# Sliding-window attention and soft MoE: value rows loaded two to a packet, keys ordered odd then even

## The chip, the cores and the metric

The kernel runs on one core of a Trainium2 chip. The metric is device time in microseconds (us) of one execution; lower is better. The engines are called as the profile calls them: PE (TensorE matmul) and PEld (its weight loads), DVE (VectorE), ACT (ScalarE), POOL (GpSimd) and SP (SyncE).

## The reference

Attention over 8 batches of 8 heads, 576 positions and 64 dimensions, in which a query sees itself and the 63 keys before it, then a soft mixture of 8 experts with 4 slots each on the 4608 tokens.

```python
scores = scale * np.matmul(q, k.transpose(0, 1, 3, 2))
mask = (rel >= 0) & (rel < window)            # window = 64
scores = np.where(mask, scores, -1000000000.0)
...
attn = attn / (np.sum(attn, axis=-1, keepdims=True) + 1e-09)
return np.matmul(attn, v).astype(np.float32)
...
logits = x @ phi                              # x: the attention's output, 4608 x 512
d = ...                                       # softmax of logits over tokens
slot_input = d.T @ x
...
h = np.maximum(slot_input[e] @ w1[e], 0.0)    # 512 -> 1024
slot_out[e] = h @ w2[e]                       # 1024 -> 512
c = ...                                       # softmax of logits over slots
return c @ slot_out
```

## The kernel before, in words

**Pairs and blocks.** Two heads of a batch are a pair; there are 32 pairs (`NP`), four to a batch. A head's 576 queries are nine blocks of 64. Block i sees the 128 keys of a window that begins 64 before the block (`kwindow`, L344). The two heads of a pair lie on partitions 0 to 63 and 64 to 127: `qb` holds the queries with zeros for the other head, so that one product with 128 weight columns gives the scores of both.

**A step of the main loop** (L556 to L635) works on several pairs at different stages, all in an order written out by hand (`manual_schedule`); every engine runs its own instructions in that order. For step n: scores of block 8 of pair n-3 (`st_score8`); transposes of the keys of pair n+1 (L319) and their copy into `kT` (`st_copy_k`, on ACT at L330, for every fourth pair on DVE at L327); attention times values of pair n-4 (`st_av`, L408) and its division (L417, L418); transposes and copies of the queries of pair n; the maxima by query (L349, L352 in PE; L356, L366 in DVE), which become an extra row of weights `rt` (L369, L370); transposes of the attention's output (`fr_transpose`, L432); scores of blocks 0 to 7 of pair n-2 by key (`st_score`: first L375, keys as weights and queries streamed, then L378, which adds mask and maximum) and the exponential (L384). Once in four steps come the logits, the softmax over tokens and the slots of a batch (`fr_logits`, `fr_dispatch`, `fr_slots`, `fr_acc`).

**The shape of a product.** A form such as 128*64 128x65 in the profile is: 128 rows and 64 columns of weights, 65 columns streamed. The transposes (96*64) and the value products (128*64) alternate between the lower and the upper 64 output partitions; scores and maxima are 128*128.

**Values.** Two pairs are a group (16 groups). `load_v` puts 18 chunks of 128 key rows of a group into `v1`, one row (64 values, float32 to float16 on the way) to a partition. For every second window the chunk boundaries lie 64 rows off; for these `shift_v` has POOL copy the two halves of each chunk into `v2` (L183, L185). A column of ones behind the values gives the sum of the weights.

**Loads.** K, q, v and most weights are loaded by DMAs that POOL issues, in the order of its instructions. In step n = 2i `loads` first takes a weight load if one is due (`WSLOTS`), then waits for and shifts the values of group i-1, then issues v of group i+1 and q of group i+3; in step 2i+1 it issues k of group i+4. POOL also does a subtraction for the softmax over slots once in four steps (L491). At the end of the loop it issues the last weights: w1 of expert 7 into the buffers of q, then the halves of w2 of experts 6 and 7 (`load_half`, L150 and L155; w2 of 6 has a tile of its own, w2 of 7 lies in the buffers of k).

**The end.** After the last pair come the slots, the first expert products (`first`, L819), the second (`second` L840, `second_last` L849, which uses the halves last loaded), and the output: products with the softmax over slots (L896), a scaling (L901, L903), and 16 stores from SP's queue (L905).

Of the kernel before, what the change touches and what calls it, by code (L numbers as in the profile page):

```python
# [12 lines left out]
ALU = mybir.AluOpType  # L13
# [5 lines left out]
def kernel(  # L19
# [21 lines left out]
    NFC = F // 128  # L41
    NRES = E - 1
    NCH = H * S // 128
    VP = 96

    ctx.enter_context(tc.manual_schedule())

# [42 lines left out]
    w1_t, w2_t = {}, {}  # L90
    for e in range(NRES):
        w1 = pwt.tile([128, NKK, F], FP16, name=f"w1_{e}")
        w2 = pwt.tile([128, NFC, D], FP16, name=f"w2_{e}")
        w1_t[e] = [w1[:, kk, :] for kk in range(NKK)]
        w2_t[e] = [w2[:, fc, :] for fc in range(NFC)]
        w1_t[e, 0], w2_t[e, 0] = w1, w2


    first_rows = {}
# [9 lines left out]
    def round_rows(tag, pr, copy):  # L109
# [1 line left out]

    ident_h = const.tile([128, 128], FP16, name="ident_h")
    nc.vector.memset(ident_h, 0.0)
    wb = const.tile([64, 128], FP16, name="wb")
    nc.vector.memset(wb, 0.0)
    make_identity(nc, ident_h, nomemset=True)
    nc.gpsimd.affine_select(out=wb, in_=wb, compare_op=ALU.is_gt, fill=NEG,
                            base=0, pattern=[[1, 128]], channel_multiplier=-1)
    nc.gpsimd.affine_select(out=wb, in_=wb, compare_op=ALU.is_ge, fill=NEG,
                            base=64, pattern=[[-1, 128]], channel_multiplier=1)  # L120
    load_k(1)


# [43 lines left out]
    v1s = [pvv.tile([128, NCH, VP], FP16, name=f"v1_{i}") for i in range(2)]  # L167
    v2s = [pvv.tile([128, NCH, 66], FP16, name=f"v2_{i}") for i in range(2)]

    def load_v(g):  # L170
        b, gq = divmod(g, 2)
        c = slice(NVC * gq, NVC * gq + NVC)
        nc.gpsimd.dma_start(out=v1s[b % 2][:, c, 0:Dh],  # L173
                            in_=v[b].rearrange("h s d -> (h s) d").rearrange("(c p) d -> p c d", p=128)[:, c, :])

    def shift_v(g):
        b, gq = divmod(g, 2)
        v1, v2 = v1s[b % 2], v2s[b % 2]
        c0, c1 = NVC * gq, NVC * gq + NVC

        w1, w2 = [t[:, :, :].rearrange("p c x -> p (c x)").bitcast(mybir.dt.int32)
                  .rearrange("p (c x) -> p c x", c=NCH)[:, :, 0:Dh // 2] for t in (v1, v2)]
        nc.gpsimd.tensor_copy(out=w2[64:128, c0:c1, :], in_=w1[0:64, c0:c1, :])  # L183
        c0 = max(c0, 1)
        nc.gpsimd.tensor_copy(out=w2[0:64, c0:c1, :], in_=w1[64:128, c0 - 1:c1 - 1, :])  # L185


    warm = v1s[1][:, 0:7, :].rearrange("p c x -> p (c x)")
    nc.vector.memset(warm, 1.0)

    def warm_up(n):
# [22 lines left out]
    nc.scalar.copy(out=lh[64:128], in_=db[64:128, 0:NB].unsqueeze(2).broadcast_to([64, NB, 128]))  # L214

    NK, NQ = 4, 3
    kTs = [pqk.tile([128, 64 + S], FP16, name=f"kT{i}") for i in range(NK)]
    qbs = [pqk.tile([128, NB, 2, 64], FP16, name=f"qb{i}") for i in range(NQ)]
    def zero_q(i):
        nc.vector.memset(qbs[i][64:128, :, 0, :], 0.0)  # L220
        nc.vector.memset(qbs[i][0:64, :, 1, :], 0.0)

    for t_ in kTs:
        nc.vector.memset(t_[:, 0:64], 0.0)
    zero_q(0)

    def no_token():
# [1 line left out]

    no_token()  # L230
    round_rows("ks", 0, nc.scalar.copy)
    nc.vector.tensor_copy(out=lh[0:64], in_=wb[:, :].unsqueeze(1).broadcast_to([64, NB, 128]))
    round_rows("qs", 0, nc.vector.tensor_copy)
    wm = const.tile([128, 5, 128], FP16, name="wm")
    for i in range(2):
        nc.vector.tensor_copy(out=wm[64 * i:64 * i + 64], in_=wb[:, :].unsqueeze(1).broadcast_to([64, 5, 128]))
    nc.vector.memset(wm[:, 0, 0:64], NEG)
    round_rows("ks", 1, nc.vector.tensor_copy)
    NR = 2
    rts = [const.tile([128, 128], FP16, name=f"rt{i}") for i in range(NR)]  # L240
# [7 lines left out]
    ms = [const.tile([128, 128], FP16, name=f"m{i}") for i in range(2)]  # L248

    def ones_v(i):  # L250
        nc.vector.memset(v1s[i][:, :, Dh:Dh + 1], 1.0)
        nc.vector.memset(v2s[i][:, :, Dh:Dh + 1], 1.0)
        nc.vector.memset(v2s[i][0:64, 0, 0:Dh], 0.0)


    phi_f = w1_t[NRES - 1, 0][:, 0, 0:2 * NKK * NSLOT].bitcast(FP32).rearrange("p (c s) -> p c s", s=NSLOT)
# [4 lines left out]
    ssf = const.tile([128, 4, 32], FP32, name="ssf")  # L261
    quarter = const.tile([128, 4], FP32, name="quarter")
    emask = const.tile([128, 2], FP32, name="emask")

    def late_constants(n):
        if n == 0:
            nc.vector.memset(ms[0], 0.0)
            zero_q(1)
        elif n == 1:
            nc.vector.tensor_tensor(out=lh[64:128, 0, 0:64], in0=lh[64:128, 0, 0:64],  # L270
                                    in1=db[64:128, 10:11].broadcast_to([64, 64]), op=ALU.add)
            make_rt(rts[0])
            nc.vector.memset(ms[1], 0.0)
            zero_q(2)
        elif n == 2:
            make_rt(rts[1])
        elif n == 3:
            ones_v(0)
        elif n == 4:
            ones_v(1)  # L280
        elif n == 5:
            nc.vector.tensor_copy(out=phi_sb, in_=phi_f)
            nc.vector.memset(quarter, 0.0)
            for d_ in ds:
                nc.vector.memset(d_[:, 192:256], 0.0)
            nc.vector.memset(nmax[1], 1.0e30)
            nc.vector.memset(stat, 0.0)
        elif n == 7:
            for t in range(4):
                nc.vector.tensor_copy(out=ss[32 * t:32 * t + 32],  # L290
                                      in_=ident_h[32 * t:32 * t + 32, 32 * t:32 * t + 32]
                                      .unsqueeze(1).broadcast_to([32, 4, 32]))
                nc.vector.memset(quarter[32 * t:32 * t + 32, t:t + 1], 1.0)
        elif n == 15:
            nc.vector.tensor_copy(out=ssf, in_=ss)
# [26 lines left out]
    def turned(tq):  # L322
        return tq[:, 0:S].rearrange("p (r g) -> p g r", r=RQ)

    def st_copy_k(p, on_vector=False):
        if on_vector:
            nc.vector.tensor_scalar(out=kTs[p % NK][:, 64:64 + S], in0=turned(a_kh), scalar1=QKS, scalar2=None,  # L327
                                    op0=ALU.mult)
        else:
            nc.scalar.activation(kTs[p % NK][:, 64:64 + S], turned(a_kh), AF.Copy, scale=QKS)  # L330

    def st_copy_q(p, both=False):
        for hf in range(2):
# [38 lines left out]
    def st_scores(p, blocks, at):  # L372
        rt = rts[p % NR]
        for i in blocks:
            nc.tensor.matmul(at(i), kwindow(p, i), qblock(p, i), start=(i % 4 == 0), stop=False,  # L375
                             skip_group_check=True)
        for i in blocks:
            nc.tensor.matmul(at(i), lh[:, i, :], rt[:, :], start=False, stop=True, skip_group_check=True)  # L378

# [19 lines left out]
    def st_av(p, a_v=a_v):  # L399
        b, hp = divmod(p, HP)  # L400
        v1, v2 = v1s[b % 2], v2s[b % 2]
        pt = pts.pop(p)
        for hf in range(2):
            for i in range(NB):
                f = NB * (2 * hp + hf) + i
                rhs = (v1 if f % 2 else v2)[:, f // 2, 0:65]
                r0 = 64 * (i % 2)
                nc.tensor.matmul(a_v[r0:r0 + 64, hf, 65 * (i // 2):65 * (i // 2) + 65],  # L408
                                 pt[:, i, 64 * hf:64 * hf + 64], rhs, start=True, stop=True, skip_group_check=True)
# [132 lines left out]
    def loads(n):  # L542
        if n in WSLOTS:
            load_w(WSLOTS[n])
        i, odd = divmod(n, 2)
        if odd:
            if 0 <= i < NG - 4:
                load_k(i + 4)
        elif i > 0:
            shift_v(i - 1)  # L550
            if i + 1 < NG:
                load_v(i + 1)
            if i + 3 < NG:
                load_q(i + 3)

    for n in range(-1, NP - 1):  # L556
        loads(n)
# [80 lines left out]
    def fill(k, bank):  # L638
        for _ in range(k):
# [2 lines left out]


    NE = 2 * S // 128
    ct4 = [v1s[0][:, 12 * i:12 * i + 12, :].rearrange("p c x -> p (c x)").rearrange("p (e x) -> p e x", e=NE)
           for i in range(3)]
    v2f = v2s[0][:, :, :].rearrange("p c x -> p (c x)")
    ct4.append(v2f[:, 0:2 * S].rearrange("p (e x) -> p e x", e=NE))
# [89 lines left out]
    fr_exp(b - 1)  # L738
    fr_transpose_copy(p - 2, a_qh)
    nc.vector.memset(a_s[:, 0, 128:192], -1.0e30)  # L740
    st_av(p)
    st_norm(p)
    th = a_mh[:, 1, 0:256]
    fr_dispatch(b - 1, th)
# [19 lines left out]
    ssf_ = ssf[:, :, :].rearrange("p t s -> p (t s)")  # L764
# [22 lines left out]
    accs = kTs[0][:, 0:D]  # L787
# [182 lines left out]
```

## Time and profile before

| | |
|---|---|
| three timed runs | median 191.71 us (190.43 to 192.57) |
| the profiled execution | 190.24 us, of which the span from the first to the last instruction is 188.2 us |
| granted TensorE clock, mean | 0.978 |
| DMA packets | 62,302, of which 38,848 under 512 B; 41.47 MB, mean 220 GB/s |
| HBM | 61.93 MB read, 9.44 MB written |
| v loads (L173) | 16 of 288 KB, 1.234 us each to issue, median 13.3 us to landing |
| k and q loads (L79) | 15 each of 288 KB, about 0.69 us each to issue, median 15.4 and 13.5 us |
| late halves of w2 (L150, L155) | 8 of 256 KB, 0.74 us each to issue, median 15.3 and 12.0 us |
| POOL copies of values (L183, L185) | 32, about 0.66 us each |
| scores by key (L375) | 256 + 32 products of 128*128 with 128 columns |

The span is divided by what happens in it: up to about 9 us the first loads, up to 134 us the main loop, up to 150 us the last pairs and the slots, up to 160 us the experts, then the output. In the profile's rows a group is a line, an engine, an operation and the tiles out<-in; "idle before" is the engine's idle time ahead of such instructions and what ended it. In a list of waits the three numbers are us in total, times and the longest. A PE duration contains the passage through the array; how fast products follow each other is read from their starts.

### The profile page before, as it was taken

How to read it: one execution, taken by the hardware profiler on the slowest of the kernel's cores; microseconds unless marked ns; L12 is line 12 of the kernel's file. 1: busy time of each engine (PE TensorE's matmuls, PEld its weight loads, DVE VectorE, ACT ScalarE, POOL GpSimd, SP SyncE). 2: the span in 40 equal slices, each digit the busy share in tenths (PEclk: the TensorE clock that was granted, in tenths of full speed). 3: DMA queues.
4: the chain of work that ended last, by engine and by line, in shares of the span. 5: the costliest groups of instructions: out<-in, count | busy, mean ns of one | idle time of the engine just before them, and what ended most of it. 6: DMA issues, size and time to landing. Idle time of an engine off the chain costs nothing.

```text
span 188.2 us, 7073 instructions
## 1 busy us (share of the span) xinstructions
PE 160.0 (85%) x3039; PEld 120.5 (64%) x3039; DVE 142.9 (76%) x354; ACT 145.0 (77%) x267; POOL 83.0 (44%) x123
## 2 busy tenths in 40 slices
PE   5777999999999999999999999999899899878400
PEld 1466778877777677777777787777785357543100
DVE  6797786897888789788888878897887734689700
ACT  6677879989889899889898898989478455589500
POOL 7955726171682453862953706707653170000000
PEclk9999999999999999999999999999999999999965
DMA  6999999999999999999999999999999999999996
GB/s 160 223 184 185 228 172 226 175 222 180 185 223 180 213 191 185 201 206 181 209 193 191 211 187 190 203 202 192 216 211 216 205 196 193 247 340 392 417 417 264
DMA packets 62302, 41.47 MB, mean 220 GB/s; under 512 B 38848, under 2 KB 58304, under 8 KB 61376
## 3 DMA queue, kind: packets, MB, share of 16 engines
q0 software_dynamic: 56560, 30.35, 116.7%
q1 hardware_dynamic: 5712, 10.68, 16.0%
q8 instruction: 23, 0.38, 0.7%
q14 instruction: 7, 0.06, 0.1%
HBM read 61.93 MB, written 9.44 MB: 379 GB/s over the span
## 4 chain that ended last, share of the span: by engine, by line
PE 45%; DVE 34%; ACT 6%; DMA 5%; issue 4%; DVEq 0%; SPq 0%; ACTq 0%
DVE m L356 10%; PE a_m L349 5%; DVE x_b L418 5%; PE a_m L352 5%; PE a_v L408 4%; PE a_s L375 4%; PE a_s L378 4%; PE a_q L319 3%; DMA out_dram<-w 3%; PE a_k L432 3%; DVE kT L327 3%; DVE rt L370 2%; DVE acc L529 2%; DMA w<-in_q_dram 2%; PE ha L819 2%
## 5 line engine op out<-in xcount | busy, mean ns | idle before, releaser
L339 ACT ACTIVATE qb<-a_q 64x576 f16<-64x576 f16 x63 | 40.6, 645 | 6.1 <-PE a_q L319 4.9
L356 DVE TENSOR_REDUCE m<-a_m 128x8 f16<-128x1024 f32 x32 | 39.1, 1223 | 1.0
L384 ACT ACTIVATE pt<-a_s 128x1024 f16<-128x1024 f32 x32 | 32.8, 1023 | 6.8 <-PE a_s L378 5.6
L183 POOL COPY v<-v 64x576 int32<-64x576 int32 x16 | 10.6, 661 | 41.1 <-DMA v<-in_v_dram 41.0
L418 DVE TENSOR_TENSOR x_b<-a_v,rc 128x640 f16<-128x640 f32 x31 | 25.6, 824 | 1.1
L352 PEld LDWEIGHTS <-qb 128*128 128x128 f16 x256 | 16.9, 98 | 7.6 <-DVE qb L336 0.3
L349 PE MATMUL a_m<-wm,ident_h 128*128 128x512 f16 x64 | 19.3, 384 | 1.4 <-DVE m L356 1.4
L378 PEld LDWEIGHTS <-lh 128*128 128x128 f16 x288 | 18.7, 98 | 2.0 <-issue 1.7
L173 POOL DMA_DIRECT2D v<-in_v_dram x16 | 19.7, 1234 | 0.0
L375 PEld LDWEIGHTS <-kT 128*128 128x128 f16 x288 | 18.6, 98 | 1.6 <-issue 1.4
L436 ACT COPY xt<-a_k 128x576 f16<-128x576 f16 x28 | 17.9, 639 | 2.2 <-PE a_k L432 0.9
L375 PE MATMUL a_s<-qb,kT 128*128 128x128 f16 x256 | 19.5, 219 | 0.0
L378 PE MATMUL a_s<-rt,lh 128*128 128x128 f16 x256 | 19.5, 219 | 0.0
L352 PE MATMUL a_m<-kT,qb 128*128 128x128 f16 x256 | 19.5, 219 | 0.0
L408 PE MATMUL a_v<-v,pt 128*64 128x65 f16 x558 | 15.6, 196 | 2.4 <-DVE m L366 1.1
L79 POOL DMA_DIRECT2D ks<-in_k_dram x15 | 10.5, 697 | 16.0 <-PE a_s L378 3.8
L370 DVE CAST rt<-a_v 9x128 f16<-9x128 f32 x30 | 8.7, 289 | 10.8 <-PE a_v L369 10.5
L408 PEld LDWEIGHTS <-pt 128*64 128x64 f16 x576 | 13.5, 110 | 4.7 <-DVE m L366 1.8
L330 ACT ACTIVATE kT<-a_k 128x576 f16<-128x576 f16 x24 | 15.7, 655 | 0.8 <-PE a_k L319 0.8
L319 PE MATMUL a_q<-ident_h,qs 96*64 96x96 f16 x384 | 14.8, 206 | 1.2 <-DVE a_q L228 1.1
L319 PE MATMUL a_k<-ident_h,ks 96*64 96x96 f16 x384 | 14.4, 212 | 1.0 <-DVE ks L110 0.8
L901 DVE TENSOR_SCALAR w<-cp,rcs 128x256 f32<-128x256 f32 (+1 forms) x24 | 13.4, 610 | 2.3 <-PE cp L896 1.9
(183 smaller groups left out, 327.8 us busy)
## 6 DMA issues: line engine op xcount, KB each, us to landing
w<-in_moe_w_dram POOLq DMA_DIRECT2D x13, 1024.0 KB, 18.0
out_dram<-w SPq DMA_DIRECT2D x8, 768.0 KB, 6.8
v<-in_v_dram POOLq DMA_DIRECT2D x16, 288.0 KB, 13.3
ks<-in_k_dram POOLq DMA_DIRECT2D x15, 288.0 KB, 15.4
qs<-in_q_dram POOLq DMA_DIRECT2D x15, 288.0 KB, 13.5
out_dram<-w SPq DMA_DIRECT2D x3, 384.0 KB, 4.0
w1h<-in_moe_w_dram POOLq DMA_DIRECT2D x4, 256.0 KB, 16.7
w<-in_moe_w_dram POOLq DMA_DIRECT2D x4, 256.0 KB, 15.3
```

The lines of the kernel that those rows point to most:

```text
L173: nc.gpsimd.dma_start(out=v1s[b % 2][:, c, 0:Dh], in_=v[b].rearrange("h s d -> (h s) d").rearrange("(c p) d -> p c d", p=128)[:, c, :])
L319: nc.tensor.transpose(tq[64 * hf:64 * hf + 64, RP * r:RP * r + RP], src[0:RP, h + hf, Dh * r:Dh * r + Dh], ident_h[0:RP, 0:RP])
L339: nc.scalar.activation(qbs[p % NQ][h, :, hf, :], turned(a_qh)[h], AF.Copy, scale=QKS)
L349: nc.tensor.matmul(a_m[:, j, :], ident_h[:, :], wm[:, j:j + 4, :].rearrange("p c x -> p (c x)"), start=True, stop=False, skip_group_check= ...
L352: nc.tensor.matmul(a_m[:, i // 4, 128 * (i % 4):128 * (i % 4) + 128], qblock(p, i), kwindow(p, i), start=False, stop=True, skip_group_chec ...
L356: nc.vector.reduce_max(ms[p % 2][:, 64:72].rearrange("p (l c) -> p l c", l=2), a_m[:, :, :].rearrange("p l (c x) -> p l c x", x=128), axis ...
L375: nc.tensor.matmul(at(i), kwindow(p, i), qblock(p, i), start=(i % 4 == 0), stop=False, skip_group_check=True)
L378: nc.tensor.matmul(at(i), lh[:, i, :], rt[:, :], start=False, stop=True, skip_group_check=True)
L384: nc.scalar.activation(st_pt(p)[:, 0:8, :].rearrange("p i x -> p (i x)"), a_s[:, :, :], AF.Exp, scale=XS)
L408: nc.tensor.matmul(a_v[r0:r0 + 64, hf, 65 * (i // 2):65 * (i // 2) + 65], pt[:, i, 64 * hf:64 * hf + 64], rhs, start=True, stop=True, skip ...
L418: nc.vector.tensor_tensor(out=xbs[b][:, :, 128 * hp:128 * hp + 128].rearrange("p c (l d) -> p l c d", l=2), in0=avv[:, :, :, 0:64], in1=rc ...
L436: nc.scalar.copy(out=xts[b][:, hp, :], in_=th[:, 0:S])
```

## The change

The values are loaded two rows (128 values) to a partition, on partitions 0 to 63 of `v1`; a packet has 256 B in place of 128 B. POOL copies the even rows to partitions 64 to 127, so that a chunk holds its odd rows below and its even rows above, and makes `v2` with four copies of 32 partitions. `kT` gets two planes, even and odd keys; the scores of a block become two products of 64 weight columns each, odd keys to output partitions 0 to 63, even ones to 64 to 127. Masks (`wb`, `wm`, `lh`) are built in that order. The shift now stands behind the load issues of its step. Since `v1` is wider, w2 of expert 6 has no tile of its own any more: it lies in `v1s[1]`, and the halves of w2 are issued behind the last value products. A float32 copy of `ss` is made by POOL late, into `kT`, instead of by DVE in step 15.

```diff
-    VP = 96
+    VP = 160
+    PL = 32 + S // 2
...
+    w2_t[NRES - 1, 0] = v1s[1][:, :, :].rearrange("p c x -> p (c x)")[:, 0:NFC * D].rearrange("p (c d) -> p c d", d=D)
...
     def load_v(g):
-        nc.gpsimd.dma_start(out=v1s[b % 2][:, c, 0:Dh],
-                            in_=v[b].rearrange("h s d -> (h s) d").rearrange("(c p) d -> p c d", p=128)[:, c, :])
+        nc.gpsimd.dma_start(out=v1s[b % 2][0:64, c, 0:2 * Dh],
+                            in_=v[b].rearrange("h s d -> (h s) d").rearrange("(c p t) d -> p c (t d)", p=64, t=2)[:, c, :])
...
     def shift_v(g):
-        nc.gpsimd.tensor_copy(out=w2[64:128, c0:c1, :], in_=w1[0:64, c0:c1, :])
-        c0 = max(c0, 1)
-        nc.gpsimd.tensor_copy(out=w2[0:64, c0:c1, :], in_=w1[64:128, c0 - 1:c1 - 1, :])
+        copy = nc.gpsimd.tensor_copy
+        copy(out=w1[64:128, c0:c1, 32:64], in_=w1[0:64, c0:c1, 0:32])
+        cp = max(c0, 1)
+        for t in range(2):
+            x = slice(32 - 32 * t, 64 - 32 * t)
+            copy(out=w2[64 * t:64 * t + 32, cp:c1, 0:32], in_=w1[32:64, cp - 1:c1 - 1, x])
+            copy(out=w2[64 * t + 32:64 * t + 64, c0:c1, 0:32], in_=w1[0:32, c0:c1, x])
...
-    kTs = [pqk.tile([128, 64 + S], FP16, name=f"kT{i}") for i in range(NK)]
+    kTs = [pqk.tile([128, 2, PL], FP16, name=f"kT{i}") for i in range(NK)]
...
-    nc.vector.memset(wm[:, 0, 0:64], NEG)
+    for i in range(2):
+        nc.vector.memset(wm[:, 0, 64 * i:64 * i + 32], NEG)
...
     def st_copy_k(p, on_vector=False):
+        out = kTs[p % NK][:, :, 32:PL].rearrange("p t (g r) -> p t g r", r=RQ // 2)
+        in_ = a_kh[:, 0:S].rearrange("p (r t g) -> p t g r", t=2, g=RP)
...
     def kwindow(p, i):
-        return kTs[p % NK][:, 64 * i:64 * i + 128]
+        return kTs[p % NK][:, :, 32 * i:32 * i + 64]
...
     def st_scores(p, blocks, at):
         for i in blocks:
-            nc.tensor.matmul(at(i), kwindow(p, i), qblock(p, i), start=(i % 4 == 0), stop=False,
-                             skip_group_check=True)
+            for hf in range(2):
+                nc.tensor.matmul(at(i)[64 * hf:64 * hf + 64, :], kwindow(p, i)[:, 1 - hf, :], qblock(p, i),
+                                 start=(i % 4 == 0), stop=False, skip_group_check=True)
...
     def st_av(p, a_v=a_v):
-                rhs = (v1 if f % 2 else v2)[:, f // 2, 0:65]
+                rhs = v1[:, f // 2, 64:129] if f % 2 else v2[:, f // 2, 0:65]
...
     def loads(n):
         elif i > 0:
-            shift_v(i - 1)
             if i + 1 < NG:
                 load_v(i + 1)
             if i + 3 < NG:
                 load_q(i + 3)
+            shift_v(i - 1)
...
     make_ss4()
-    for d in range(2):
-        load_half(d)
...
+    nc.gpsimd.tensor_copy(out=ssf_, in_=ss[:, :, :].rearrange("p t s -> p (t s)"))
     st_av(p)
+    for d in range(2):
+        load_half(d)
     st_norm(p)
```

More of the change, by code (lines that the diff above doesn't have):

```diff
@@ L92 @@
         w1 = pwt.tile([128, NKK, F], FP16, name=f"w1_{e}")
-        w2 = pwt.tile([128, NFC, D], FP16, name=f"w2_{e}")
         w1_t[e] = [w1[:, kk, :] for kk in range(NKK)]
-        w2_t[e] = [w2[:, fc, :] for fc in range(NFC)]
-        w1_t[e, 0], w2_t[e, 0] = w1, w2
+        w1_t[e, 0] = w1
+        if e < NRES - 1:
+            w2 = pwt.tile([128, NFC, D], FP16, name=f"w2_{e}")
+            w2_t[e] = [w2[:, fc, :] for fc in range(NFC)]
+            w2_t[e, 0] = w2
     first_rows = {}
@@ L113 @@
     nc.vector.memset(ident_h, 0.0)
-    wb = const.tile([64, 128], FP16, name="wb")
+    wb = const.tile([64, 2, 2, 32], FP16, name="wb")
     nc.vector.memset(wb, 0.0)
@@ L117 @@
     nc.gpsimd.affine_select(out=wb, in_=wb, compare_op=ALU.is_gt, fill=NEG,
-                            base=0, pattern=[[1, 128]], channel_multiplier=-1)
+                            base=0, pattern=[[1, 2], [64, 2], [2, 32]], channel_multiplier=-1)
     nc.gpsimd.affine_select(out=wb, in_=wb, compare_op=ALU.is_ge, fill=NEG,
-                            base=64, pattern=[[-1, 128]], channel_multiplier=1)
+                            base=64, pattern=[[-1, 2], [-64, 2], [-2, 32]], channel_multiplier=1)
+    wb = wb[:, :, :, :].rearrange("p t h x -> p (t h x)")
     load_k(1)
@@ L167 @@
     v1s = [pvv.tile([128, NCH, VP], FP16, name=f"v1_{i}") for i in range(2)]
+    w2_t[NRES - 1, 0] = v1s[1][:, :, :].rearrange("p c x -> p (c x)")[:, 0:NFC * D].rearrange("p (c d) -> p c d", d=D)
+    w2_t[NRES - 1] = [w2_t[NRES - 1, 0][:, fc, :] for fc in range(NFC)]
     v2s = [pvv.tile([128, NCH, 66], FP16, name=f"v2_{i}") for i in range(2)]
@@ L181, in shift_v @@
         w1, w2 = [t[:, :, :].rearrange("p c x -> p (c x)").bitcast(mybir.dt.int32)
-                  .rearrange("p (c x) -> p c x", c=NCH)[:, :, 0:Dh // 2] for t in (v1, v2)]
-        nc.gpsimd.tensor_copy(out=w2[64:128, c0:c1, :], in_=w1[0:64, c0:c1, :])
-        c0 = max(c0, 1)
-        nc.gpsimd.tensor_copy(out=w2[0:64, c0:c1, :], in_=w1[64:128, c0 - 1:c1 - 1, :])
-    warm = v1s[1][:, 0:7, :].rearrange("p c x -> p (c x)")
+                  .rearrange("p (c x) -> p c x", c=NCH) for t in (v1, v2)]
+        copy = nc.gpsimd.tensor_copy
[5 more added lines that the diff above has]
+            copy(out=w2[64 * t + 32:64 * t + 64, c0:c1, 0:32], in_=w1[0:32, c0:c1, x])
+    warm = v1s[1][:, 0:4, :].rearrange("p c x -> p (c x)")
     nc.vector.memset(warm, 1.0)
@@ L223 @@
     for t_ in kTs:
-        nc.vector.memset(t_[:, 0:64], 0.0)
+        nc.vector.memset(t_[:, :, 0:32], 0.0)
     zero_q(0)
@@ L231 @@
     round_rows("ks", 0, nc.scalar.copy)
-    nc.vector.tensor_copy(out=lh[0:64], in_=wb[:, :].unsqueeze(1).broadcast_to([64, NB, 128]))
+    for i in range(2):
+        nc.vector.tensor_copy(out=lh[0:64, :, 64 * i:64 * i + 64],
+                              in_=wb[:, 64 - 64 * i:128 - 64 * i].unsqueeze(1).broadcast_to([64, NB, 64]))
     round_rows("qs", 0, nc.vector.tensor_copy)
@@ L235 @@
     for i in range(2):
-        nc.vector.tensor_copy(out=wm[64 * i:64 * i + 64], in_=wb[:, :].unsqueeze(1).broadcast_to([64, 5, 128]))
-    nc.vector.memset(wm[:, 0, 0:64], NEG)
+        nc.vector.tensor_copy(out=wm[64 * i:64 * i + 64], in_=wb.unsqueeze(1).broadcast_to([64, 5, 128]))
+    for i in range(2):
+        nc.vector.memset(wm[:, 0, 64 * i:64 * i + 32], NEG)
     round_rows("ks", 1, nc.vector.tensor_copy)
@@ L250, in ones_v @@
     def ones_v(i):
-        nc.vector.memset(v1s[i][:, :, Dh:Dh + 1], 1.0)
+        nc.vector.memset(v1s[i][:, :, 2 * Dh:2 * Dh + 1], 1.0)
         nc.vector.memset(v2s[i][:, :, Dh:Dh + 1], 1.0)
-        nc.vector.memset(v2s[i][0:64, 0, 0:Dh], 0.0)
+        nc.vector.memset(v2s[i][0:32, 0, 0:Dh], 0.0)
+        nc.vector.memset(v2s[i][64:96, 0, 0:Dh], 0.0)
     phi_f = w1_t[NRES - 1, 0][:, 0, 0:2 * NKK * NSLOT].bitcast(FP32).rearrange("p (c s) -> p c s", s=NSLOT)
@@ L260 @@
     ss = const.tile([128, 4, 32], FP16, name="ss")
-    ssf = const.tile([128, 4, 32], FP32, name="ssf")
     quarter = const.tile([128, 4], FP32, name="quarter")
@@ L269, in late_constants @@
         elif n == 1:
-            nc.vector.tensor_tensor(out=lh[64:128, 0, 0:64], in0=lh[64:128, 0, 0:64],
-                                    in1=db[64:128, 10:11].broadcast_to([64, 64]), op=ALU.add)
+            for i in range(2):
+                lh_ = lh[64:128, 0, 64 * i:64 * i + 32]
+                nc.vector.tensor_tensor(out=lh_, in0=lh_, in1=db[64:128, 10:11].broadcast_to([64, 32]), op=ALU.add)
             make_rt(rts[0])
@@ L294, in late_constants @@
         elif n == 15:
-            nc.vector.tensor_copy(out=ssf, in_=ss)
             nc.vector.memset(emask, 0.0)
@@ L325, in st_copy_k @@
     def st_copy_k(p, on_vector=False):
+        out = kTs[p % NK][:, :, 32:PL].rearrange("p t (g r) -> p t g r", r=RQ // 2)
+        in_ = a_kh[:, 0:S].rearrange("p (r t g) -> p t g r", t=2, g=RP)
         if on_vector:
-            nc.vector.tensor_scalar(out=kTs[p % NK][:, 64:64 + S], in0=turned(a_kh), scalar1=QKS, scalar2=None,
-                                    op0=ALU.mult)
+            nc.vector.tensor_scalar(out=out, in0=in_, scalar1=QKS, scalar2=None, op0=ALU.mult)
         else:
-            nc.scalar.activation(kTs[p % NK][:, 64:64 + S], turned(a_kh), AF.Copy, scale=QKS)
+            nc.scalar.activation(out, in_, AF.Copy, scale=QKS)
     def st_copy_q(p, both=False):
@@ L644 @@
     NE = 2 * S // 128
-    ct4 = [v1s[0][:, 12 * i:12 * i + 12, :].rearrange("p c x -> p (c x)").rearrange("p (e x) -> p e x", e=NE)
+    ct4 = [v1s[0][:, 8 * i:8 * i + 8, :].rearrange("p c x -> p (c x)")[:, 0:2 * S].rearrange("p (e x) -> p e x", e=NE)
            for i in range(3)]
@@ L740 @@
     nc.vector.memset(a_s[:, 0, 128:192], -1.0e30)
+    ssf_ = kTs[1][:, :, :].rearrange("p t x -> p (t x)")[:, 0:256].bitcast(FP32)
+    nc.gpsimd.tensor_copy(out=ssf_, in_=ss[:, :, :].rearrange("p t s -> p (t s)"))
     st_av(p)
+    for d in range(2):
+        load_half(d)
     st_norm(p)
@@ L763 @@
     nc.vector.tensor_scalar(out=bd, in0=quarter, scalar1=new[:, :], scalar2=None, op0=ALU.mult)
-    ssf_ = ssf[:, :, :].rearrange("p t s -> p (t s)")
     mg = a_q[:, 128:136]
@@ L786 @@
     nc.vector.tensor_tensor(out=fac, in0=fac, in1=wt, op=ALU.mult)
-    accs = kTs[0][:, 0:D]
+    accs = kTs[0][:, :, :].rearrange("p t x -> p (t x)")[:, 0:D]
     nc.vector.tensor_scalar(out=accs[:, 0:256], in0=acc[:, 0:256], scalar1=fac[:, :], scalar2=None, op0=ALU.mult)
```

## The prediction

> **What bounds the kernel now.** I read the page first, then the waits, the chain of waits over one period of the main loop, the timeline of TensorE beside it, and last the landings of the late loads. The page:
>
> ```profile
> PE 160.0 (85%) x3039; PEld 120.5 (64%) x3039; DVE 142.9 (76%) x354; ACT 145.0 (77%) x267; POOL 83.0 (44%) x123
> DMA  6999999999999999999999999999999999999996
> PE 45%; DVE 34%; ACT 6%; DMA 5%; issue 4%; DVEq 0%; SPq 0%; ACTq 0%
> ```
>
> Two things are full at once. The DMA engines are busy in every slice, yet the chain that ended last is PE and DVE with 79% of the span, and DMA has 5% of it. So the loads run just fast enough. The waits say who feels the DMA:
>
> ```profile
> POOL v L183 <- DMA v<-in_v_dram: 41.0, 14, 5.5
> DVE rt L370 <- PE a_v L369: 10.5, 21, 0.8
> ACT pt L384 <- PE a_s L378: 5.6, 18, 1.7
> ```
>
> GpSimd idles 41.0 us for the values, but no engine is listed as waiting for what it then copies. DVE and ACT wait for PE. In the loop four pairs make a period, 17.1 us (the same scores are on the chain at 74.76 and 91.90). The chain inside one:
>
> ```profile
> 90.75 0.67 DVE kT L327
> ...
> 91.47 0.44 PE a_k L432 x5
> 91.90 0.45 PE a_s L375 x8
> 92.35 0.45 PE a_s L378 x8
> 92.80 0.11 PE a_q L507 x2
> 92.91 0.06 PE a_k L375
> 92.97 0.06 PE a_k L378
> 93.02 0.38 PE a_k L319 x12
> ...
> 95.52 0.45 PE a_s L375 x8
> 95.97 0.45 PE a_s L378 x8
> ```
>
> From 91.47 to 97.1 us the chain is PE alone, product after product: two calls of the eight-block scores (L375, L378) and one of the block-8 scores lie on it in each period. Whatever lengthens these calls lengthens the kernel. What a call costs after the change is read from this timeline of TensorE (start, duration, then line, array shape and count):
>
> ```profile
> 97.06 0.22 PE L378 MATMUL a_k<-rt,lh 128*128 128x128 f16 x1
> 97.21 0.45 PE L319 MATMUL a_k<-ident_h,ks 96*64 96x96 f16 x12
> 97.49 0.48 PE L408 MATMUL a_v<-v,pt 128*64 128x65 f16 x18
> 98.17 0.45 PE L319 MATMUL a_q<-ident_h,qs 96*64 96x96 f16 x12 [0.20 <-DVE a_q L228]
> 98.55 0.60 PE L349 MATMUL a_m<-wm,ident_h 128*128 128x512 f16 x2
> ```
>
> Starts count here, not durations. Full-width products of 128 columns start 0.055 us apart (eight in 0.45). From one of them to the first half-width one (97.06 to 97.21) it is 0.15: 0.10 more. Twelve half-width transposes take 0.28 when another half-width group follows (97.21 to 97.49), but 0.38 when a full-width one follows (98.17 to 98.55): again 0.10. So each change between widths stops PE for about 0.10 us.
>
> **The scores, the part that counts.** L375 becomes two products of 64 weight columns per block, between full-width neighbours (L432 or L507 before, L378 behind).
> - The products themselves: six pairs of 96-column transposes take 0.28, 0.49 ns a column and pair, so the two halves run beside each other. A pair at 128 columns is 0.062, eight are 0.50 against 0.45: +0.05.
> - Two width changes: +0.20. Together 0.25 for an eight-block call, 0.20 for block 8.
>
> By the Trainium skill, TensorE: Matmul & The Clock Gate, section LDWEIGHTS, a weight load takes its column count over 1.2 in ns: 53 for 64 columns, an estimate, so two loads could not hide under a pair and an eight-block call would gain 0.4 us more. The trace disagrees: in the same stretch 17 loads of 64 columns (L408) took 0.36 us, 21 ns each.
>
> Calls on the chain, counted in its list in order of time: eight-block scores at 25.23 and twice in each of six periods, then 139.75, is 14 x 0.25 = 3.5. (134.32 follows half-width products; there a change is only moved.) Block 8 at 15.39, 18.18, 29.84, once a period, and 140.64 is 10 x 0.20 = 2.0, and 138.59 adds one change, 0.1. In the other steps PE waits before the value products for a maximum (transposes from 118.01, 0.28 long, L408 only at 118.64). That swallows 0.35 of the 0.45 added; in four periods the rest is on the chain: 0.1 x 4 = 0.4. Sum +6.0.
>
> **The value loads.** Each falls from 2304 packets to 1152. In 30 to 130 us the full engines (1600 engine-us) moved 39,585 packets and 19.42 MB, in 146 to 160 us (224) 4,024 and 2.75 MB. Two equations give about 2 ns a packet and 78 us a MB (a small difference of two near rates), so 18,432 packets fewer are worth 18,432 x 2 ns / 16 = 2.3 us over the whole kernel. The bounds are 0 and half of the values' whole time, 4.7 MB x 78 us / 16 / 2 = 12 us. None of it lies on the chain: worth 0 in the loop.
>
> **GpSimd.** Five copies replace two. Each covers 576 elements a lane, the row L183 (661 ns); that row has 64 partitions, two of the new forms 32, and I take the same: 3.3 us a group for 1.3. The v issue (1.23) falls towards the k issue (0.70) with its packets; I take 0.9. In two steps (8.5 us) GpSimd then has 3.3 + 0.9 + 0.69 (q) + 0.70 (k) + 0.45 (weights) + 0.25 (L491) = 6.3 us. The copies move behind the v and q issues. Those now wait for PE to free buffers (the value products of group i-3, the q transposes of group i-1, both in step 2i-1) and no longer for a landing. Behind them queue the copies, L491 and the next k issue. The copies end about 6 us after that step's value products; the first value products that need them come three steps (12.8 us) later, L491's reader also three steps after its issue, k is four groups ahead. Cost 0, cover about 6 us.
>
> **VectorE, ScalarE, start.** The kT copies (655 and 746 ns) write two planes in runs of three. The reads already jumped at each element, and L339 with its split output costs 645 for 576: taken as 0. Upper end a half more, 0.35 x 7 = 2.4 us of DVE copies on the chain. One more memset (0.11) at 6.8 us: +0.1. The cast removed at n=15 and the split one-off copies are small: 0.
>
> **The late weights.** The eight half loads now wait for the last value products (before at 141.75 to 142.3, then about 148) and for one GpSimd copy. Before, the last was issued at 153.25 and took about 10 us; its products start at 163.43, as it lands. After: eight issues of 0.74 and 2.1 MB at 197 GB/s, 10.6 us, after 2 us to the first: by 161 all, by 156 the first four. They are needed at 163.4 + 6 and 157.7 + 6. Cost 0, cover about 8 us; L491 behind them is free at 154 as before. The output no longer shares the engines with the last two halves: of its first pieces' delays I take back 0.4.
>
> **Sum.** 190.24 (the profiled execution; span 188.2) + 6.0 + 0.1 - 0.4 = **195.9 us**. The three timed runs have a median 1.5 us above the profiled one; I read that as loads landing late in a kernel that uses them as they land, which the slack above ends. If it is something else, 197.4.
>
> **Rivals.**
> - *The stops are covered (12%).* Half of the calls prove not to bind, as in the steps with the 0.38 us wait: +2.7, 192.9, within 1%. Against it: PE has no gap in the stretch shown.
> - *The loads bind, and the change wins (6%).* DMA is full, the last half is used as it lands, and the timed runs lie above the profile. If the stops cost nothing, 190.24 - 0.4 = 189.8 or a little less. Against: no PE wait on a landing after the start.
> - *The halves do not overlap (7%).* 16 x 0.055 = 0.90 a call, 0.45 more: 14 x 0.4 more than forecast, 201.5. The overlap of L319 and L408 speaks against it. By the Trainium skill's weight-load rule above the time would be much the same.
> - *GpSimd is late or blocks DVE (8%).* If a copy costs half more, two steps need 8.0 us of 8.5; beyond 8.5 each us is paid in some 14 groups: 198 to 203. By the Trainium skill, SBUF — State Buffer, section SBUF: two separate sides, GpSimd and a DVE instruction that uses the shared port pair lock each other out for a whole instruction. The trace has L183 at 657 to 664 ns in all 16, so no lock shows here; with 80 copies it could.
> - *The kT copies cost half more (5%)*: 198.3.
>
> **Chances and range.** The forecast has 62%, its own range 193.9 to 198. A measurement here tells 1% from no change: 189.8 to 193.6 around 191.71. Faster: the second rival, 0.06. Same: the first and the forecast's low edge, 0.15. Slower: 0.79. Leaving out the fastest tenth and the slowest, 192.3 to 199.5.
>
> **What would show it.** PE starts 0.15 apart between L432 and the first score product and between the last and L378; sixteen halves in about 0.5 us; a period of 17.8 to 17.9 us for 17.1; more PE and less DVE in the chain. GpSimd's wait for v near zero; DMA slices below 9 in the loop; half loads landed before 162. Wrong: no gap at the width changes, waits of PE on GpSimd's v copies, or on a weight landing.

## The result and the profile after

| | before | after |
|---|---|---|
| median of 6 runs | 190.92 us (190.33 to 192.57) | 203.9 us (201.63 to 205.25) |
| profiled execution, span | 190.24 us, 188.2 us | 205.25 us, 203.5 us |
| DMA packets, of which under 512 B | 62,302, 38,848 | 43,874, 20,416 |

The changed kernel is slower: the ratio is 1.0595, 95% interval 1.0518 to 1.0671, some 11 us. Three of the six runs after, the profiled one among them, are slow ones (over 1.5% above the fastest), so the ratio is of the other three, and sums made on the profiled execution are one to three us too high. Its page, busy time by engine, DMA share in 40 slices and the chain's shares:

```profile
PE 173.3 (85%) x3327; PEld 125.0 (61%) x3327; DVE 144.2 (71%) x358; ACT 145.0 (71%) x267; POOL 109.9 (54%) x172
...
DMA  6999999999999999999999999999999990499994
...
PE 64%; DVE 16%; issue 5%; DMA 5%; ACT 3%; POOL 1%; SPq 0%; DVEq 0%; ACTq 0%
```

PE has 288 products and 288 weight loads more, and its share of the chain rises from 45% to 64%. DMA still shows a 9 in every slice of the loop, with 30% fewer packets. The list of waits (total, times, longest):

```profile
ACT pt L403 <- PE a_s L397: 16.7, 30, 2.1
...
PEld L394 <- issue: 4.8, 9, 1.6
...
PE a_s L394 <- issue: 2.2, 2, 1.5
...
PE a_q L465 <- issue: 2.0, 1, 2.0
```

GpSimd's copies no longer wait for the landing of values (41.0 us before; now rows of 3.4 and 1.0 us stand ahead of its load issues), and ACT's exponential waits three times as long for PE (16.7 us for 5.6). New are waits of PE and of its weight loads for "issue", that is, for nothing the profile shows, of up to 2.0 us; the longest such row before is 1.2. The change of widths is seen in the timeline of PE around one call (start, duration, line, shape, count):

```profile
102.91 0.33 PE L451 MATMUL a_k<-ident_h,x_b 128*128 128x128 f16 x3
103.17 0.64 PE L394 MATMUL a_s<-qb,kT 128*64 128x128 f16 x16
103.74 0.62 PE L397 MATMUL a_s<-rt,lh 128*128 128x128 f16 x8
```

From the first half-width product to the first full-width one behind it there is 0.57 us, where eight full-width ones took 0.45: 0.42 for sixteen halves (28 ns each on the mean) and a gap of 0.15. The two halves do run beside each other. This much is as forecast. What is not, is in the chain of waits between 89 and 98.5 us:

```profile
89.11 0.54 PE a_m L367 x2
...
89.87 0.96 issue
90.84 0.38 PE a_m L370 x4
...
96.15 0.51 PE a_s L394 x13
96.66 1.48 issue
98.14 0.27 PE a_s L394 x3
```

PE stops in the middle of a group, four of eight products done, thirteen of sixteen done, with nothing to wait for. From the end of one stop to the end of the next there are 7.30 us. The windows (length, busy time and count of PE, then of its weight loads, and on to granted clock, DMA share, which sums the times of the packets and so can pass 1, and GB/s) of that stretch, of the one before it, and of a later one:

```profile
83.54:90.84 7.30, 6.26 (x129) 4.51 (x128) 4.68 (x10) 5.70 (x10) 4.01 (x7) 1.00 1.76 172
90.84:98.14 7.30, 5.78 (x129) 4.50 (x128) 6.06 (x17) 4.82 (x9) 5.64 (x9) 1.00 1.39 194
...
100.00:102.00 2.00, 2.00 (x29) 1.33 (x24) 1.63 (x3) 1.36 (x4) 1.39 (x2) 0.50 1.53 200
```

Between two stops PE has executed 128 products and 128 weight loads (one product runs across each edge): blocks of 256 instructions. All four stops of 0.7 us or more in the loop fit this: counted from the first product, with a weight load to each, they lie behind instruction 1214, 2750, 3262 and 3518, which is 190 plus a multiple of 256 each time. The page has a queue of instructions, here after and then before:

```profile
q8 instruction: 26, 0.43, 0.8%
```

```profile
q8 instruction: 23, 0.38, 0.7%
```

That is 26 packets of 16.5 KB (0.43 MB / 26) for 23, and 2 x 3327 instructions are 26.0 blocks of 256, 2 x 3039 are 23.7. So each packet brings PE one block, 64 B an instruction. In the part of the DMA view from 83.54 to 87.9 us no such packet is listed; from 87.9 to 90.84 us, this:

```profile
DMA packets 980, 0.50 MB, mean 170 GB/s; under 512 B 555, under 2 KB 976, under 8 KB 976
...
q8 instruction: 1, 0.02, 3.0%
```

3.0% of 16 engines over 2.94 us is 1.4 us for the packet. By its record it began at 87.94, 4.4 us after the block began, landed at 89.33, and PE went on at 90.84. Before, the blocks of the loop between 38 and 76 us have packets that begin 3.5 to 4.1 us in and take about 1 us, and PE begins the next block 1.3 to 1.9 us after the landing; that is 6.2 to 6.6 us for 256 instructions. Before uses 670 instructions in a period of 17.0 us, 256 in 6.5; it stood just at that edge. The change makes them 742 (2 x 36 more).

The last of the window rows has the clock at 0.50: behind the 1.48 us stop, from 99.5 to 102.9 us, products run at up to twice their time, about 1.4 us in all. By the Trainium skill, TensorE: Matmul & The Clock Gate, section Part 1, the array's clock halves after an idle window of about 3.4 us; no stop here is that long, so as a length of idle time the row does not bear that out. Nor does the length of a stop decide it alone: behind the stop of 2.00 us at 37.28 in the same execution the clock stayed at 1.00. What else it takes no run shows.

In the profiled executions the loop from the DVE copy of kT at 24.07 (after: 25.45) to that at 124.53 (137.52) takes 11.6 us more. The four stops of 0.7 us or more on the chain there (37.28, 76.02, 89.87 and 96.66) sum to 5.2, the halved clock is 1.4, and the width changes are some 4 by the runs below, together 10.6.

### The profile page after: what moved, and what is told of

Same layout as the page of the kernel before. It is cut to its first block, busy times and chain, and to the rows that moved or that the text cites. A ratio compares the mean times of both kernels' runs of the same rounds, so it can differ in the third digit from the quotient of the medians.

```text
span 203.5 us, 7712 instructions
## 1 busy us (share of the span) xinstructions
PE 173.3 (85%) x3327; PEld 125.0 (61%) x3327; DVE 144.2 (71%) x358; ACT 145.0 (71%) x267; POOL 109.9 (54%) x172
## 2 busy tenths in 40 slices
DMA packets 43874, 41.52 MB, mean 204 GB/s; under 512 B 20416, under 2 KB 39872, under 8 KB 42944
## 4 chain that ended last, share of the span: by engine, by line
PE 64%; DVE 16%; issue 5%; DMA 5%; ACT 3%; POOL 1%; SPq 0%; DVEq 0%; ACTq 0%
PE a_s L394 8%; PE a_s L397 8%; PE a_m L367 7%; PE a_m L370 6%; PE a_k L336 4%; PE a_k L451 4%; PE a_q L336 4%; PE a_v L427 4%; DVE x_b L437 3%; DMA w<-in_k_dram 3%; DMA out_dram<-w 2%; DVE acc L548 2%; DVE m L374 2%; PE a_k L394 2%; DVE kT L346 2%
## 5 line engine op out<-in xcount | busy, mean ns | idle before, releaser
L403 ACT ACTIVATE pt<-a_s 128x1024 f16<-128x1024 f32 x32 | 32.8, 1025 | 16.7 <-PE a_s L397 16.7
L182 POOL DMA_DIRECT2D v<-in_v_dram x16 | 14.0, 872 | 26.4 <-PE a_v L427 10.5
L394 PEld LDWEIGHTS <-kT 128*64 128x64 f16 x576 | 19.2, 109 | 10.4 <-issue 4.8
L370 PEld LDWEIGHTS <-qb 128*128 128x128 f16 x256 | 17.8, 101 | 9.7 <-issue 1.9
L394 PE MATMUL a_s<-qb,kT 128*64 128x128 f16 x512 | 20.6, 222 | 2.2 <-issue 2.2
L198 POOL COPY v<-v 32x576 int32<-32x576 int32 x32 | 21.2, 664 | 1.4
L197 POOL COPY v<-v 32x544 int32<-32x544 int32 (+1 forms) x32 | 20.8, 650 | 1.6
L370 PE MATMUL a_m<-kT,qb 128*128 128x128 f16 x256 | 20.6, 225 | 1.1 <-issue 1.0
L397 PEld LDWEIGHTS <-lh 128*128 128x128 f16 x288 | 17.4, 97 | 5.1
L455 ACT COPY xt<-a_k 128x576 f16<-128x576 f16 x28 | 17.9, 640 | 3.6 <-PE a_k L451 2.6
L397 PE MATMUL a_s<-rt,lh 128*128 128x128 f16 x256 | 19.8, 220 | 0.0
L336 PE MATMUL a_q<-ident_h,qs 96*64 96x96 f16 x384 | 15.8, 212 | 0.8 <-DVE a_q L242 0.3
L923 ACT ACTIVATE w<-cp,rcs 128x256 f32<-128x256 f32 (+1 forms) x24 | 12.5, 585 | 3.4 <-PE cp L916 3.2
## 6 DMA issues: line engine op xcount, KB each, us to landing
w1h<-in_moe_w_dram POOLq DMA_DIRECT2D x4, 256.0 KB, 11.6
```

Of the source, the lines that this page charges most:

```text
L197: copy(out=w2[64 * t:64 * t + 32, cp:c1, 0:32], in_=w1[32:64, cp - 1:c1 - 1, x])
L198: copy(out=w2[64 * t + 32:64 * t + 64, c0:c1, 0:32], in_=w1[0:32, c0:c1, x])
L336: nc.tensor.transpose(tq[64 * hf:64 * hf + 64, RP * r:RP * r + RP], src[0:RP, h + hf, Dh * r:Dh * r + Dh], ident_h[0:RP, 0:RP])
L370: nc.tensor.matmul(a_m[:, i // 4, 128 * (i % 4):128 * (i % 4) + 128], qblock(p, i), kwindow(p, i), start=False, stop=True, skip_group_chec ...
L394: nc.tensor.matmul(at(i)[64 * hf:64 * hf + 64, :], kwindow(p, i)[:, 1 - hf, :], qblock(p, i), start=(i % 4 == 0), stop=False, skip_group_c ...
L403: nc.scalar.activation(st_pt(p)[:, 0:8, :].rearrange("p i x -> p (i x)"), a_s[:, :, :], AF.Exp, scale=XS)
```

## The experiments

The theories at the start: the split of the scores costs the time, by its widths or by its number of instructions, against the rest of the change (values, GpSimd, late weights).

**The split alone, in the kernel before.**

```diff
-            nc.tensor.matmul(at(i), kwindow(p, i), qblock(p, i), start=(i % 4 == 0), stop=False,
-                             skip_group_check=True)
+            for hf in range(2):
+                nc.tensor.matmul(at(i)[64 * hf:64 * hf + 64, :], kwindow(p, i)[:, 64 * hf:64 * hf + 64], qblock(p, i),
+                                 start=(i % 4 == 0), stop=False, skip_group_check=True)
```

> The kernel before, with the scores of a block in two half-width products and nothing else changed. Theory A (the change's cost lies in TensorE alone: two changes of width per call, and more instructions than the instruction fetch delivers beside full DMA engines): 200 to 205 us against 191, width gaps of 0.15 us, and some waits of 0.5 us or more that the profile calls issue. Rival B (the values' loads, their five copies or the late weights cost most): 196 us or less, and no such waits beyond those of before.

Measured: 200.53 us, ratio 1.0504 (1.043 to 1.0577). Most of the loss comes with the split alone, without anything that the values need.

**All of the change but the split.** One product of 128 keys per block, read as they lie in `kT`, so the order of keys in the scores is not that of the values.

```diff
-            for hf in range(2):
-                nc.tensor.matmul(at(i)[64 * hf:64 * hf + 64, :], kwindow(p, i)[:, 1 - hf, :], qblock(p, i),
-                                 start=(i % 4 == 0), stop=False, skip_group_check=True)
+            nc.tensor.matmul(at(i), kTs[p % NK][:, :, :].rearrange("p t x -> p (t x)")[:, 32 * i:32 * i + 128],
+                             qblock(p, i), start=(i % 4 == 0), stop=False, skip_group_check=True)
```

> The changed kernel with the scores of a block in one product of 128 weight columns again, read as they lie in memory, so keys are out of order: that part of the computation is changed, the amount of work is that of before. Theory A: 189.5 to 192 us, no long issue waits. Rival B: 197 us or more.

Measured: 193.0 us, ratio 1.0149 (1.0111 to 1.0187), a little above theory A's range. The rest of the change gains nothing, and loses some 2.6 us. In the profiled executions 1.44 us of that are there at the first kT copy of the loop (25.51 for 24.07), 0.95 come in the loop, 0.4 behind it. At the start the chain of waits of this run has:

```profile
15.40 0.67 POOL v L193
...
18.18 0.68 POOL v L198
...
18.89 0.45 PE a_v L426 x15
19.34 0.29 PE a_q L336 x12
19.63 0.74 PE a_m L367 x2
20.37 0.85 PE a_m L370 x8
```

The first value products follow five copies on GpSimd, which end the chain's GpSimd part at 18.85. PE had paused 1.04 us shortly before, for ACT, and its timeline gives 0.47 us for this wait; behind the two the clock is halved from 19.8 until 23.2 us (0.74 and 0.85 us for rows that take 0.54 and 0.45). The list of waits of this run has:

```profile
PE a_v L426 <- POOL v L198: 1.2, 3, 0.5
```

Two of these three waits for GpSimd's copies are in the loop, 0.34 us ahead of the value products at 35.88 and 0.38 ahead of those at 53.29. PE also stands for "issue" for 0.40 us until 40.33 and 0.17 until 46.80, behind instruction 1214 and 1470, at the edges that stop the changed kernel too. These four sum to 1.3 us, enough for the 0.95 of the loop; which of them it consists of is not shown.

**More products, no change of width.** In the kernel before, each score product is cut by its queries into two full-width ones of 64 columns: as many instructions as the split has, in the same places.

```diff
-            nc.tensor.matmul(at(i), kwindow(p, i), qblock(p, i), start=(i % 4 == 0), stop=False,
-                             skip_group_check=True)
+            for l in range(2):
+                nc.tensor.matmul(at(i)[:, 64 * l:64 * l + 64], kwindow(p, i), qblock(p, i)[:, 64 * l:64 * l + 64],
+                                 start=(i % 4 == 0 and l == 0), stop=False, skip_group_check=True)
```

> The kernel before, with each score product cut by queries into two full-width products of 64 streamed columns: as many TensorE instructions as in the changed kernel, no change of width. Theory A1 (the fetch of instructions is short in itself): long issue waits at multiples of 256 instructions, 194 to 199 us. Rival A2 (the width changes alone do it, the long waits are their consequence): 191 to 193 us and no long issue waits. If weight loads of 128 columns do not keep up with 64 streamed columns, each eight-block call grows by up to 0.2 us, about 2 us in all, which the starts of L375 will show.

Measured: 199.98 us (197.9 to 202.2 in four runs), ratio 1.0501 (1.0427 to 1.0576), about as slow as the split, and at or above the upper end of what was expected of the instructions alone. Yet sixteen of these products take 0.47 us in the chain where eight took 0.45. What they cost is seen in its windows, cut where its stops end:

```profile
35.83:42.30 6.47, 6.06 (x129) 4.94 (x129) 4.71 (x10) 5.64 (x12) 3.73 (x5) 1.00 1.54 206
42.30:48.49 6.19, 5.67 (x130) 4.49 (x128) 4.82 (x12) 5.60 (x10) 1.33 (x3) 1.00 1.48 185
48.49:54.96 6.47, 5.41 (x128) 4.26 (x128) 4.37 (x9) 5.36 (x10) 5.66 (x9) 1.00 1.61 199
```

256 instructions again, in 6.2 to 6.5 us, the last of it a stop of 0.5 to 1 us. The edges lie behind instruction 1214, 1470, 1726 and 1982, by the same count as in the changed kernel. The theory became: the supply of PE's instructions, a packet for each 256 beside load queues that are full, sets the rate of the loop. It can be tried by freeing the DMA engines with the instructions unchanged.

**Fewer weight loads.** Of the 13 whole loads of experts' weights only the four of the first two experts stay (nine are left out, not ten as the expectations say), and the others' products use these; so the experts' output differs. The same edit in the kernel before, in the one with more products, in the changed one:

```diff
         second, e = divmod(i, NRES)
+        if e > 1:
+            return
...
-        return w2_t[e][d][fc] if e == last else w2_t[e][fc][:, DH * d:DH * d + DH]
+        return w2_t[e][d][fc] if e == last else w2_t[e if e == last - 1 else e % 2][fc][:, DH * d:DH * d + DH]
...
-                                 w1_t[4 * g + j][kk][:, 512 * f2:512 * f2 + 512],
+                                 w1_t[last if 4 * g + j == last else j % 2][kk][:, 512 * f2:512 * f2 + 512],
```

> The kernel before with 10 of its 13 whole weight loads left out: experts 0 to 5 (for w1 0 to 6) use the weights of experts 0 and 1, so the experts' part of the computation is changed. It is the baseline for the next two. Its loop was not held up by loads: 187 to 191 us by theory A and by rival B.

Measured: 189.74 us, ratio 0.9948 (0.9912 to 0.9985). Relief of the DMA alone is worth 1 us to the kernel before: its loads don't bind.

> The same leaving out, with each score product cut by queries into two full-width ones (288 more products, no change of width). Theory F (the instruction fetch is late because its DMA stands behind full load queues): within 2 us of the kernel before with fewer weights, long issue waits gone. Rival G (256 instructions cannot come faster than in 6.2 us whatever the DMA engines do): 8 to 10 us above it, the waits as before.

Measured: 195.47 us, ratio 1.0223 (1.0137 to 1.0308), 5.7 above the kernel before with fewer weights: between the two theories. Of the 9.6 us that the products cost beside full queues, some 4 are gone. The chain shows where. In the first stretch the queues are still full, in the second, from about 57 us, not (kT copies of two successive periods, with the stops between):

```profile
42.34 0.68 DVE kT L329
...
49.47 0.89 issue
...
55.92 0.91 issue
...
60.86 0.68 DVE kT L329
77.64 0.67 DVE kT L329
94.70 0.67 DVE kT L329
```

Beside full queues a period has 18.5 us, with stops; behind them 16.8 and 17.1, as before the change, with the same 742 instructions and no stop of 0.4 us or more on the chain until 141 us. Of the 5.7 us in the profiled executions, 4.3 have come by the copy at 60.86, the next four periods add 0.1 (67.7 us for 67.6), and some 1.3 come at the end. Its windows, cut at the blocks of 256, on both sides of that point:

```profile
43.78:50.35 6.57, 5.69 (x134) 4.50 (x131) 4.88 (x12) 5.85 (x10) 5.14 (x7) 1.00 1.70 186
50.35:56.82 6.47, 5.41 (x128) 4.26 (x128) 4.37 (x9) 5.21 (x9) 3.62 (x5) 1.00 1.86 182
63.08:68.43 5.35, 5.15 (x130) 4.07 (x130) 4.21 (x13) 5.04 (x9) 2.02 (x4) 1.00 1.36 152
68.43:74.22 5.79, 5.64 (x133) 4.66 (x131) 4.41 (x12) 5.37 (x10) 3.40 (x5) 1.00 1.13 103
74.22:80.15 5.93, 5.48 (x132) 4.65 (x130) 5.77 (x14) 5.18 (x12) 2.87 (x4) 1.00 0.87 83
86.13:91.66 5.53, 5.25 (x132) 4.45 (x130) 4.32 (x13) 5.09 (x11) 2.67 (x5) 1.00 1.21 110
```

A block takes 6.5 us where the DMA engines move 185 GB/s of small packets, and 5.4 to 5.9 in the four rows with room, where no stop ends it. The packets of instructions begin 3.5 to 4.3 us into a block in the first part and mostly 0 to 2.6 us in the second.

> The changed kernel with the same weight loads left out. Theory F: 5 to 8 us above the kernel before with fewer weights (the width changes on the chain, and the start), long issue waits gone. Rival G: 11 to 13 us above, with the waits.

Measured: 199.75 us, ratio 1.0449 (1.0383 to 1.0516), 10.0 above the kernel before with fewer weights, more than theory F's 5 to 8 and less than G's 11 to 13. The changed kernel has two long stops in its loop's chain (36.8 and 51.6 us) and none behind; it gets back 3 to 4 us as well. Behind 62 us its periods are 17.5 to 17.7, 0.65 above those of before.

**The widths alone.** The split in the kernel before, with the same edit of the weights: the pair of this and of the run of 195.47 has the same instructions in the same places, and only the widths differ.

> The kernel before with its scores by key in two half-width products per block, and without 10 of the 13 whole loads of experts' weights (those experts use the weights of the first two, so the output differs). It has the same number of TensorE instructions in the same places as the run with the products cut by queries and fewer weights (195.5 us, periods of 16.8 to 17.1 us once its stalls end at 57 us); only the widths differ, so the difference of the two is the price of the width changes with the supply of instructions the same. Theory 1 (a period pays 0.65 us for them, as the changed kernel with fewer weights showed with 17.5 to 17.7 us): periods of 17.5 to 17.7 us after 60 us, 198 to 200 us. Theory 2 (the prediction's 0.8 us per period and 6 us in all): 17.8 to 17.9 us, 200.5 to 202. Theory 3 (the changed kernel's longer periods came from its other parts, GpSimd's copies or the values): 16.8 to 17.1 us as without the widths, 195 to 196.5.

Measured: 199.45 us, ratio 1.0437 (1.0381 to 1.0493): 4.0 us for the widths. Its kT copies in the chain:

```profile
60.94 0.68 DVE kT L329
78.45 0.67 DVE kT L329
96.14 0.68 DVE kT L329
```

17.5 and 17.7 us; over the four periods to 131.34 the mean is 17.6, against 16.9 for the run without the widths: 0.68 a period. It also stands level with the changed kernel of 199.75 us: with room in the queues, the values, GpSimd's copies and the late weights cost nothing that can be told.

**The copies ahead of the load issues.** The run with whole scores, with the shift put back in its place.

```diff
         elif i > 0:
+            shift_v(i - 1)
             if i + 1 < NG:
                 load_v(i + 1)
             if i + 3 < NG:
                 load_q(i + 3)
-            shift_v(i - 1)
```

> The changed kernel with one product of 128 keys per block (keys read as they lie in memory, so the order of keys in the scores is not the values' order), and with the copies of the values put back ahead of the load issues of their step. The run with whole scores alone took 193.0 us, and its chain has the first value products (L426 at 18.89) behind five GpSimd copies from 15.40 on, then products at about half their rate until 23.7. Theory 1 (those first copies cost the 1.4 us by which that run was late at 25 us): the copies start earlier, the chain holds fewer than five copies of GpSimd ahead of the first value products, the DVE copy that was at 25.51 comes at 24.0 to 24.6, and the time is 191 to 192. Theory 2 (the order of copies and issues doesn't matter; the five copies simply take 3.3 us wherever they start): 25.3 to 25.6 again and 192.5 to 193.5. Theory 3 (in the loop the load issues, now behind copies that wait for value products, come late): 193.5 to 196, with TensorE waits on k or q landings.

Measured: 194.41 us, ratio 1.0187 (1.0097 to 1.0276): the time of the third theory, but without waits of TensorE on k or q. In DVE's timeline the first kT copy of the loop starts at 24.84, at 25.43 with the shift last and at 23.98 in the kernel before, so 0.59 of 1.45 us of the late start are gained (the pause of 1.04 us is there, the one for GpSimd not, and the clock holds), but GpSimd waits again for the landing of the values, as the list of waits says:

```profile
POOL v L193 <- DMA v<-in_v_dram: 26.3, 11, 4.0
```

With whole scores and the shift last, that row has 4.1. One such landing, copied by 52.8 us, is on the chain that ended last, and the value products follow it after a wait of 1.36 us. The order gives back later what it gains at the start; the two runs' intervals overlap.

**The halves beside the transposes.** In the changed kernel the half-width score products of blocks 0 to 7 move behind the query transposes, which are half-width too, so two width changes a call vanish.

```diff
+    def st_halves(p, blocks, at):
...
+        if live(n - 2) and not early:
+            st_halves(n - 2, range(8), s_at)
...
-            st_score(n - 2)
+            st_score(n - 2, early)
```

> The changed kernel with the sixteen half-width score products of blocks 0 to 7 moved ahead in the step, right behind the query transposes, which are half-width too (the products with mask and maximum stay where they were). The same instructions, but two changes between widths fewer on each of the 30 or so calls that move. Theory 1 (the changes of width cost 0.10 us each and lie on the chain): up to 14 calls x 0.2 = 2.8 us less than the changed kernel, 200.5 to 202.5. Theory 2 (the supply of instructions sets the rate in the loop, about 6.2 us for 256 of TensorE's while the DMA engines are full, whatever the widths): the gaps go, the issue stalls grow by what they gave, the periods of the loop stay near 18 us, and the time is 203 to 205. Theory 3 (the scores' accumulation starts earlier and its buffer is still being read by ScalarE's exponential): a new wait of TensorE on ACT, 204 or more.

Measured: 203.53 us, ratio 1.0648 (1.0576 to 1.0721): no gain, and within the second theory's range. Sixteen halves now take 0.45 us in the chain. But the product of block 8 writes `a_k`, and the moved products were the work that covered ACT's copy out of it. The chain after another stop:

```profile
95.58 0.91 issue
96.49 0.34 PE a_k L458 x3
...
96.91 0.65 ACT xt L462
...
97.60 0.25 PE a_k L393 x2
```

That copy (0.65 us) is on the chain nine times, and there are still stops of 0.4 to 1 us. A wait on ACT was among the theories, though on another of its instructions; how much of the gain went to it and how much to the supply stays open.

## Why the prediction was wrong

The forecast was 195.9 us in 192.3 to 199.5, the sign right, the time 8 us too short. By the runs of the parts alone, the split costs 10.1 us where 6.0 were forecast, and the rest of the change costs 2.6 where a gain of 0.3 was.

- **The step that failed** is "The products themselves: six pairs of 96-column transposes take 0.28, 0.49 ns a column and pair, so the two halves run beside each other. A pair at 128 columns is 0.062, eight are 0.50 against 0.45: +0.05." As streaming time that is right (0.42 for sixteen). But 288 products with their weight loads are 576 instructions, 72 a period, and what it costs to bring them to PE was not in the sum. Alone, without any width change, they made the kernel before slower by 9.6 us; with the queues relieved, by 5.7 over the relieved kernel before (195.47 - 189.74), and by nothing where the queues had room. No rival had this mechanism. Three rows that bear on it were shown: PE's count x3039, "issue 4%" in the chain, and DMA at 9 in every slice, which the prediction took for a statement on the loads alone. The row of the instruction queue, q8, has no part in it.
- **The width changes**: right in kind, place and single price (0.10 us ahead of the call and 0.12 for the call with the gap behind it, 0.22 where 0.25 was forecast). As a term, 0.8 a period were forecast and 0.68 measured with the same number of instructions; 6.0 in all were forecast and 4.0 measured with the queues relieved. Beside full queues the stops swallow most of them: the split takes 200.53 us and the cut by queries 199.98, the same within their intervals, and in the profiled executions their loops take 108.7 and 107.4 us. So the two prices don't add.
- **Period** forecast 17.8 to 17.9: it is 17.6 without stops, and 17.4 to 21.3 with them in the changed kernel, the longest with the stops of 0.96 and 1.48 us and the halved clock.
- **The value loads, 0**: no gain shows, as forecast. (The two equations give 1.6 ns a packet, not 2, so the 2.3 us would be 1.9.) But "DMA slices below 9 in the loop" was wrong; with 18,432 packets fewer the slices still show 9.
- **GpSimd, 0**: right in the prices, five copies of 0.65 to 0.66 us, the v issue at 0.87 (0.9 forecast), and no lock with DVE in sight. The cover of 6 us is not always there: in the run with whole scores PE waits for the copies of three groups, 0.47 us at the start and 0.34 and 0.38 in the loop. In the changed kernel's profile PE waits for no copy, so the rival with GpSimd late, "in some 14 groups", fell. How the 2.6 us of the run with whole scores divide beyond the start stays open.
- **kT copies, 0**: right (ACT 652 ns on the mean, DVE 747, where before had 655 and 746).
- **Late weights, 0 with 8 us of cover**: right. They landed from 159.9 to 168.7 in an execution 13 us later than before, and the last were used at 177.7, 9 us after.
- **The output, -0.4**: the stretch from the first expert products to the end is 38.8 us against 37.9; the gain did not come.
- **The rivals.** Halves that don't overlap would have given 201.5, near the time measured, but the 28 ns for each exclude it: a time can be met by the wrong mechanism. The loads do not bind, as the 1 us of the relieved kernel before shows. The stops at width changes are not covered; they cost 0.68 of the forecast 0.8.

## What to carry to other kernels

An instruction added to an engine has to be delivered too: count PE's instructions, products and weight loads, per microsecond and compare the rate with the pace at which blocks of them arrive while the loads run, here 256 in 6.2 to 6.5 us. Waits for "issue" that cut a group of like products in two, at equal counts of instructions, are the sign of it; in these runs they came beside full DMA queues and ceased where the queues had room. To price a change, run its parts alone and also once with the shared resource relieved, since two costs that lie on the same stop do not add.

## What the runs showed that was not expected

- PE's instructions come by DMA while the kernel runs, in packets of 16.5 KB for 256 of them. The packet takes mostly 0.9 to 1.5 us, is used 1.3 to 1.7 us after it has landed where PE stands waiting for 0.6 us or more, and begins mostly 3 to 4.8 us into a block beside full queues, 0 to 2.6 with room. Why it begins so late beside full queues (one at a time, and behind what) no run shows. That the stops end some 1.5 us behind these packets, each at the edge of a block of 256, is a coincidence in time, seen at each; that they need both the instructions and the full queues is shown by the runs.
- A stop of 1.48 us, and two pauses of 1.04 and 0.47 us close together, were each followed by some 3.4 us at a clock of 0.50; a pause of 1.04 us alone was not, and neither were stops of 2.00 us (the changed kernel, 37.28) and 1.45 us (the same with fewer weights, 36.80). Why, no run shows.
- Sixteen 64-column products that alternate between the halves of the output start within 0.42 us, 28 ns each on the mean, so a pair costs what one of 128 columns does.
